# A written table in place of a greedy planner for the order of every engine

## The chip, the cores and the metric

The kernel runs on one core of one Trainium2 chip. The core has a matrix engine (PE, TensorE), a vector engine (DVE), an activation engine (ACT), a general engine (POOL, GpSimd) and a queue engine (SP). Each of them works through its own instructions in the order in which the program was written; they meet through semaphores. Matrix products land in PSUM, which has eight banks here: two for tiles named h, one each for y, u, x and z, and a pair named s. Before a bank can be used again, DVE or ACT has to copy its contents out ("evict" it).

The metric is the time of one execution on the device in microseconds, the median of several runs. Before the change it is 303.93 us (three runs, 302.88 to 303.95).

## What is computed

Attention with two kinds of sliding window, then a two-layer network with silu between the layers. Eight batches of 576 positions, eight heads of 64; the first four heads see the last 32 positions, the other four see every fourth of the last 128.

```python
def _attn_ref(q, k, v):
    scores = scale * np.matmul(q, k.transpose(0, 1, 3, 2))
    rel = pos[:, None] - pos[None, :]
    mask_plain = (rel >= 0) & (rel < 32)
    mask_dil = (rel >= 0) & (rel < 128) & (rel % 4 == 0)
    scores = np.where(masks[None], scores, -1e9)
    attn = softmax(scores)
    return np.matmul(attn, v)

def _moe_ref(x, w_in, w_out):          # x: 4608 x 512
    h = x @ w_in                       # 512 -> 2048
    g = h * (1.0 / (1.0 + np.exp(-h)))
    return g @ w_out                   # 2048 -> 512
...
x = attn_out.transpose(0, 2, 1, 3).reshape(4608, 512)
```

## The kernel before

The work is cut into 598 matrix steps and some steps without a product. The names below are those of the table in the change, and the prediction's steps can be found by them.

Attention, batch b of 8. Batches 0 to 2 load q and k in natural order and transpose them on PE (`trans_a`, `trans_b`, `trans_d` and their forms for batch 0: steps TA, TB, TD, TS, TR); batches 3 to 7 are cast into scratch memory by DMAs that POOL issues (`issue_cast`) and come back transposed by DMAs that SP issues (`issue_turn`, step T). `scores` (S, seven sets for the first three batches, six for the others) makes a block of scores in two banks, ACT takes the exp of it (L702 for a pair of banks in one instruction, L706 for each bank alone), and DVE multiplies by the mask (L712). In batch 0 the mask is added by a product with the identity (L681). `av_p` and `av_d` (P and D) multiply with v; DVE then takes a reciprocal and normalises (L742, L743). `x_p` and `x_d` (XP and XD) transpose the result into xA, the input of the network, and DVE or ACT copies it there (L571 on ACT, L573 on DVE). For batches 5 to 7 this transposition goes through memory and a DMA on SP (steps W and X). `vd_of` (V) copies v; `loads_gen` (L) issues the loads of a later batch behind two copies to a `fence` tile on POOL, which wait for the transposed loads of the batch before.

The network works on ten groups of tokens, two of 256 and eight of 512. `layer1` makes 16 pieces of 128 hidden channels for each group (steps l, L976). The eviction has two forms: a silu on ACT (L985), or a tanh on ACT (L988) with a product on DVE (L990). Exp and tanh share ACT's table; silu needs another, so a change from one to the other costs a table load. Groups 8 and 9 use Strassen's scheme with seven products of half size (`l1_fast`, L1078), and so does the second layer from group 2 on (`layer2_fast`, steps y with products 0 to 6, L1210; evictions at L1230, L1237 and L1240). The scheme needs sums of weights (`w_sums` and `w_last`, steps w and v; `wa_sums`, steps a, on POOL), of xA (`xt_sums`, t) and of the hidden values (`g_sums`, u, on DVE, for group 8 on POOL), at L1166 and L1027. The second layer of groups 0 and 1 is plain (`layer2`, L1130).

What sets the order is a planner in the kernel's own text. Each step is a generator that writes its products, then yields the name of an engine and an assumed time, and is sent on when that time has come in the plan. `Plan` keeps a clock for each engine and for each bank ring; `flush` decides between ACT and DVE ("ANY") by which would end first, and between tanh and silu ("L1") by which table is loaded. The main loop holds the attention's steps, the first layer's and the second layer's in three queues and picks at each point the first candidate that is ready, under limits on how far ACT and DVE may be behind:

```python
            r = max(r, plan.t + plan.backlog(it[1].uses) - lim)
            if r <= plan.t:
                pick = q_, it
                break
```

Assumed times for loads (`LOAD_US`, `AT_W0`) stand in place of their landings. Output tiles are stored by the ACT queue, from group 7 on by SP's (`BYSP`). The bank of a step is one of the free rings it may use; the second layer alternates between y and u.

Of the kernel before, what the change touches and what calls it, by code (L numbers as in the profile page):

```python
# [10 lines left out]
F32 = mybir.dt.float32  # L11
AF = mybir.ActivationFunctionType
# [4 lines left out]
def kernel(  # L17
# [43 lines left out]
    LOOK1 = 6  # L61
    BYSP = 7
    STAG = 2.5
# [4 lines left out]
    LOAD_US = {"w": 2.57, "o": 2.57, "d": 3.2, "p": 3.0, "r": 2.3, "v": 2.57, "k0": 2.2, "r0": 1.0, "v0": 2.3, "w0a": 1.3, "w0b": 1.3}  # L68
    AT_W0 = 11.4
# [3 lines left out]
    gtp = ctx.enter_context(tc.tile_pool(name="gtp", bufs=2))  # L73
    o32 = ctx.enter_context(tc.tile_pool(name="o32", bufs=2))
    obp = ctx.enter_context(tc.tile_pool(name="obp", bufs=3))
    dram = ctx.enter_context(tc.tile_pool(name="dram", bufs=1, space=bass.MemoryType.DRAM))
    ps_h = ctx.enter_context(tc.tile_pool(name="ps_h", bufs=2, space=bass.MemoryType.PSUM))
# [64 lines left out]
    pair_tmp = {  # L142
        "hh": [as32[0][:, HT * i : HT * (i + 1)] for i in range(4)] + [as32[2][:, :GT]],
        "xz": [as32[1][:, HT * i : HT * (i + 1)] for i in range(4)] + [as32[3][:, :GT]],
        "s": [as32[4][:, HT * i : HT * (i + 1)] for i in range(3)]
        + [as32[3][:, GT : GT + HT], as32[2][:, GT : 2 * GT]],
    }
# [126 lines left out]
    AT, AT_WIN = {}, {}  # L274
    at = AT_W0
    for what in ORDER:
# [24 lines left out]
        at += LOAD_US[what] if what in LOAD_US else LOAD_US[kind]  # L301
        AT[what] = at
        if kind == "w":
            for f in range(f0, f1):
                AT_WIN[4 * n + f] = at

    def third_batch():
        for n in range(2, PEB):
            issue_nat(n, 0, H)
        issue_vraw(2)  # L310
        issue_vp(2)
        issue_cast(PEB)
        yield "DMA", 0.0

    RINGS = {"h": 2, "y": 1, "u": 1, "s": 1, "x": 1, "z": 1}
    TABLE = 1.28
    HOP = 0.18
    OVER = {"ACT": 0.105, "DVE": 0.085}
    LAT = {"ACT": 0.15, "DVE": 0.125}
    SWITCH = 0.095  # L320
    LEAN = 0.1
    ORD = 1

    class Step:
        def __init__(self, make, pe, rings=(), deps=(), uses=()):
            self.make, self.pe, self.rings, self.deps, self.uses = make, pe, rings, deps, uses
            self.after = self.keep = self.done = self.mate = self.behind = None
            self.started = False
            self.freed = None
            self.mode = 128  # L330

    class Plan:
        def __init__(self):
            self.t = 0.0
            self.now = 0.0
            self.mode = 128
            self.free = {"ACT": 5.7, "DVE": 6.6, "POOL": 0.0}
            self.table = "exp"
            self.late = False
            self.soon = lambda: True  # L340
            self.sets = {}
            self.heap = []
            self.n = 0
            self.rings = {nm: [] for nm in RINGS}

        def push(self, step, gen, ready, value=None):
            self.now = ready
            try:
                eng, us = gen.send(value)
            except StopIteration:  # L350
                step.done = ready
                return
            heapq.heappush(self.heap, (ready, self.n, step, gen, eng, us))
            self.n += 1

        def flush(self):
            while self.heap and self.heap[0][0] <= self.t:
                ready, _, step, gen, eng, us = heapq.heappop(self.heap)
                if eng == "DMA":
                    heapq.heappush(self.heap, (ready + us, self.n, step, gen, "LANDED", 0.0))  # L360
                    self.n += 1
                    continue
                if eng == "LANDED":
                    self.push(step, gen, ready)
                    continue
                mode = None
                if eng in ("EXP", "L1", "SILU"):
                    mode = "silu" if eng == "SILU" else "exp"
                    if eng == "L1" and (self.table == "silu" or not self.soon()):
                        mode = "silu"  # L370
                    if mode == "silu" or eng == "EXP":
                        us += TABLE * (self.table != mode)
                        self.table = mode
                    eng = "ACT"
                if eng == "ANY":
                    ends = {e: max(ready, self.free[e]) + n for e, n in us.items()}
                    eng = min(ends, key=ends.get)
                    us = us[eng]
                hop = HOP
                if self.late:  # L380
                    us -= OVER.get(eng, 0.0)
                    hop = LAT.get(eng, HOP)
                end = max(ready, self.free[eng]) + us
                self.free[eng] = end
                self.push(step, gen, end + hop, mode or eng)

        def wait(self, step):
            wait = [d if isinstance(d, float) else d.done for d in step.deps]
            return None if None in wait else max(wait, default=0.0)

        def ready(self, step):
            wait = self.wait(step)
            if wait is None or step.behind and not step.behind.started:
                return None
            slots = [self.slot(nm) for nm in step.rings]
            slots = [x for x in slots if x is not None]
            if step.rings and not slots:
                return None
            return max(wait, min(slots, default=0.0))

        def slot(self, nm):
            done = [0.0]
            for c in set(nm):
                ring = self.rings[c]
                more = len(ring) - RINGS[c]
                done += [u.freed or u.done for u in ring[max(0, more) : max(0, more + nm.count(c))]]
            return None if None in done else max(done)

        def start(self, step):
            step.started = True  # L410
            self.t = max(self.t, self.ready(step))
            if step.pe and step.mode != self.mode:
                self.t += SWITCH
                self.mode = step.mode
            self.flush()
            ring = None
            if step.rings:
                slots = [(self.slot(nm), i) for i, nm in enumerate(step.rings)]
                ring = step.rings[min(x for x in slots if x[0] is not None)[1]]
                for c in ring:  # L420
                    self.rings[c].append(step.keep or step)
            self.t += step.pe
            self.push(step, step.make(ring), self.t + HOP + 0.02 * self.late)
            if step.after:
                step.after()

        def backlog(self, engs):
            return max((self.free[e] - self.t for e in engs), default=0.0)

    plan = Plan()  # L430
    t2 = at
    AT_DIL = {0: 6.1, 1: AT["d1"], 2: t2 + 7.0}
    AT_PLAIN = {0: 9.3, 1: AT["p1"], 2: t2 + 7.0}
    AT_VRAW = {0: 10.1, 1: AT["r1"], 2: t2 + 8.6}
    AT_VP = {0: 11.4, 1: AT["v1"], 2: t2 + 11.4}
    AT_CAST = t2 + 18.0
    AT_REST = AT["k0"]
    AT_V1 = AT["r0"]
    AT_VP1 = AT["v0"]
    AT_WOUT = [AT[f"o{n}"] for n in range(4)]  # L440

    POOLS = {"h": ps_h, "x": ps_x, "y": ps_y, "u": ps_y, "z": ps_z}
    readers = {}
    counts = {}

    def count(key, n, then):
        counts[key] = counts.get(key, 0) + 1
        if counts[key] == n:
            then()

    def at_t(then):
        plan.now = plan.t
        then()
# [50 lines left out]
    def loads_need(b):  # L504
        return 1 + (b > PEB or b == 3)
# [914 lines left out]
```

## Time and profile before

| | |
|---|---|
| median of three runs | 303.93 us |
| span of the profiled execution | 301.1 us |
| own time of the profiled execution outside its span | not shown; the median lies 2.8 us above this span |
| mean granted TensorE clock | 0.998 |
| PE, DVE, ACT, POOL busy | 289.0, 215.4, 194.7, 97.5 us |
| ACT table loads | 12, of 1.28 us each |
| output stores | 24 on ACT's queue, 12 on SP's |

The span goes from the first instruction to the last. A row of the windows gives a stretch, its length, then for each engine the busy time and the number of instructions, the granted clock, the share of the DMA engines' time and the rate. A row of the timeline or of the chain gives start, length, engine, line, tile and count; what stands in square brackets is the idle time before it and what ended it. The engines over time, in 40 equal slices and tenths:

```profile
PE   6889999989999999999999999999999999999995
...
DVE  6388999889957784768664787576667685599511
ACT  7677783478687766766765675667665496398320
POOL 8954814000640051005000669701600069800000
```

The attention of batches 0 to 2, with both small groups, fills about the first eleven slices; the Strassen groups of the first layer stand in slices 31 to 36.

### The profile page before, as it was taken

How to read it: one execution, taken by the hardware profiler on the slowest of the kernel's cores; microseconds unless marked ns; L12 is line 12 of the kernel's file. 1: busy time of each engine (PE TensorE's matmuls, PEld its weight loads, DVE VectorE, ACT ScalarE, POOL GpSimd, SP SyncE). 2: the span in 40 equal slices, each digit the busy share in tenths (PEclk: the TensorE clock that was granted, in tenths of full speed). 3: DMA queues.
4: the chain of work that ended last, by engine and by line, in shares of the span. 5: the costliest groups of instructions: out<-in, count | busy, mean ns of one | idle time of the engine just before them, and what ended most of it. 6: DMA issues, size and time to landing. Idle time of an engine off the chain costs nothing.

```text
span 301.1 us, 7429 instructions
## 1 busy us (share of the span) xinstructions
PE 289.0 (96%) x2922; PEld 203.6 (68%) x2922; DVE 215.4 (72%) x598; ACT 194.7 (65%) x427; POOL 97.5 (32%) x135
## 2 busy tenths in 40 slices
PE   6889999989999999999999999999999999999995
PEld 3558765644567666666775577568657888888884
DVE  6388999889957784768664787576667685599511
ACT  7677783478687766766765675667665496398320
POOL 8954814000640051005000669701600069800000
PEclk9999999999999999999999999999999999999999
DMA  7999999999999949897999999943113301200231
GB/s 106 184 199 198 202 192 193 209 203 190 95 159 186 218 68 167 164 219 107 168 268 181 151 195 246 223 81 111 54 30 106 111 2 64 77 2 0 90 121 72
DMA packets 100106, 42.26 MB, mean 140 GB/s; under 512 B 68584, under 2 KB 95464, under 8 KB 100072
## 3 DMA queue, kind: packets, MB, share of 16 engines
q0 software_dynamic: 48528, 19.86, 54.6%
q1 hardware_dynamic: 48088, 15.64, 26.6%
q10 hardware_dynamic: 3456, 6.29, 6.4%
q8 instruction: 23, 0.38, 0.5%
q14 instruction: 11, 0.09, 0.1%
HBM read 39.81 MB, written 17.10 MB: 189 GB/s over the span
## 4 chain that ended last, share of the span: by engine, by line
PE 81%; DVE 9%; ACT 4%; DMA 2%; issue 1%; POOL 1%; ACTq 0%; POOLq 0%
PE y L1210 30%; PE h L976 28%; PE h L1078 8%; PE y L1130 4%; PE s L693 3%; PE av_d L739 3%; DMA nat<-in_q_dram 2%; DVE gT L990 2%; PE av_p L739 2%; DVE probs L712 1%; ACT th L988 1%; DVE oP L743 1%; ACT probs L702 1%; PE xp L785 1%; DVE oD L743 1%
## 5 line engine op out<-in xcount | busy, mean ns | idle before, releaser
L976 PE MATMUL h<-xA,w_in 128*128 128x512 f16 (+1 forms) x512 | 110.4, 352 | 1.8 <-ACT probs L706 0.9
L985 ACT ACTIVATE gT<-h 128x512 f16<-128x512 f32 x84 | 49.6, 597 | 29.1 <-PE h L976 28.3
L976 PEld LDWEIGHTS <-w_in 128*128 128x128 f16 x512 | 45.2, 97 | 32.6 <-issue 2.5
L1210 PEld LDWEIGHTS <-gT 128*128 128x128 f16 x512 | 49.0, 98 | 7.3 <-issue 0.2
L1210 PE MATMUL y<-w_out,gT 128*128 128x256 f16 x384 | 48.2, 273 | 0.0
L1210 PEld LDWEIGHTS <-work 128*128 128x128 f16 x384 | 37.0, 98 | 7.1 <-issue 1.2
L1237 DVE TENSOR_TENSOR ob<-y,nat 128x256 f32<-128x256 f32 x48 | 20.1, 422 | 24.4 <-PE y L1210 18.5
L513 POOL COPY fence<-kqT 128x1 f16<-128x1 f16 x10 | 3.2, 329 | 93.2 <-DMA kqT<-kq_s 93.2
L1210 PE MATMUL y<-w_sum,work 128*128 128x256 f16 x256 | 32.0, 273 | 0.6 <-ACT nat L1230 0.6
L739 PEld LDWEIGHTS <-probs 128*128 128x128 f16 x448 | 22.9, 98 | 13.1 <-DVE oP L743 1.7
L702 ACT ACTIVATE probs<-s 128x768 f16<-128x768 f32 (+2 forms) x31 | 24.5, 791 | 6.4 <-PE s L693 3.6
L743 DVE TENSOR_TENSOR oD<-av_d,rcps 72x256 f16<-72x256 f32 x64 | 26.9, 421 | 2.2
L1230 ACT COPY nat<-y 128x256 f32<-128x256 f32 x48 | 18.0, 384 | 11.4 <-PE y L1210 10.1
L988 ACT ACTIVATE th<-h 128x256 f32<-128x256 f32 (+1 forms) x44 | 19.2, 445 | 7.4 <-PE h L976 4.7
L990 DVE SCALAR_TENSOR_TENSOR gT<-th,h 128x256 f16<-128x256 f32 (+1 forms) x44 | 20.6, 487 | 2.2 <-ACT th L988 2.1
L742 DVE RECIPROCAL rcps<-av_d 72x4 f32<-72x4 f32 x64 | 11.1, 173 | 14.8 <-PE av_d L739 14.7
L706 ACT ACTIVATE probs<-s 128x288 f16<-128x288 f32 (+2 forms) x40 | 18.6, 487 | 4.4 <-ACT ob L1240 1.3
L743 DVE TENSOR_TENSOR oP<-av_p,rcps 96x256 f16<-96x256 f32 x48 | 20.2, 421 | 1.6
L1240 ACT COPY ob<-y 128x256 f32<-128x256 f32 x16 | 5.9, 371 | 22.9 <-PE y L1210 20.3
L712 DVE TENSOR_TENSOR probs<-probs,mask_p 128x768 f16<-128x768 f16 x21 | 12.2, 584 | 10.3 <-ACT probs L702 7.5
L739 PE MATMUL av_d<-vd,probs 128*128 128x65 f16 x256 | 16.5, 194 | 0.6 <-ACT probs L706 0.3
L1210 PE MATMUL y<-w_out,work 128*128 128x256 f16 x128 | 16.6, 273 | 0.0
(129 smaller groups left out, 486.2 us busy)
## 6 DMA issues: line engine op xcount, KB each, us to landing
out_dram<-ob ACTq DMA_DIRECT2D x24, 256.0 KB, 4.7
out_dram<-ob SPq DMA_DIRECT2D x12, 256.0 KB, 2.0
kq_s<-in_k_dram POOLq DMA_DIRECT2D x5, 576.0 KB, 9.6
kq_s<-in_q_dram POOLq DMA_DIRECT2D x5, 576.0 KB, 13.6
vp<-in_v_dram POOLq DMA_DIRECT2D x7, 384.0 KB, 8.1
w_out<-in_moe_w_out_dram POOLq DMA_DIRECT2D x4, 512.0 KB, 10.4
vraw<-in_v_dram POOLq DMA_DIRECT2D x8, 224.0 KB, 5.4
w_in<-in_moe_w_in_dram POOLq DMA_DIRECT2D x3, 512.0 KB, 9.8
```

The lines of the kernel that those rows point to most:

```text
L702: nc.scalar.activation(p2, both[:, :, :n], AF.Exp, scale=scale)
L706: nc.scalar.activation(p2[:, i], sp[i][:, :n], AF.Exp, scale=scale)
L739: nc.tensor.matmul(a[:, i, : D + 1], lhs(i), rhs(i), start=True, stop=True)
L743: nc.vector.tensor_tensor(o, a[:n, :, :D], rcp[:n, :, None].broadcast_to([n, HN, D]), ALU.mult)
L976: nc.tensor.matmul(h[:, :w], w_in16[:, c, f * P : (f + 1) * P], x_g[:, c], start=(c == 0), stop=(c == HP - 1),)
L985: nc.scalar.activation(gTs[g][:, f, :w], h[:, :w], AF.Silu, scale=2.0)
L988: nc.scalar.activation(th[:, :w], h[:, :w], AF.Tanh)
L990: nc.vector.scalar_tensor_tensor(gTs[g][:, f, :w], th[:, :w], 1.0, h[:, :w], ALU.add, ALU.mult)
L1078: nc.tensor.matmul(y, lhs[:, c, j], rhs[:, c], start=first and c == 0, stop=c == 1, skip_group_check=not first,)
L1210: nc.tensor.matmul(y, lhs[:, c, tb * P : (tb + 1) * P], rhs[:, c], start=first and c == 0, stop=c == KP - 1, skip_group_check=not first,)
L1230: nc.scalar.copy((t1, t5, u2)[n], y)
L1237: nc.vector.tensor_tensor(half, y, (u2, t5, t1)[n - 3], ALU.add)
```

## The change

The planner goes: the class `Plan` with its clocks, rings and limits, the assumed times of loads, engines and hops, the three queues and the picking loop. In its place stands `TABLE`, a text of some 1,600 words, each the name of a step, with what it is given behind "=". The words are carried out from first to last:

```python
    for token in TABLE.split():
        name, _, what = token.partition("=")
        steps[name].go(what)
```

The first word of a step with products writes them, into the bank that it names (a and b are the two h banks, s the pair). Each further word lets the step write one more piece: an eviction on ACT (A) or DVE (D), a first-layer eviction as silu (s) or as tanh with a product (t), an output store on SP's queue (S) or else on ACT's. So the order of each engine, the bank, the evicting engine, the form and the queue are all written down. The start, the middle and the end of the table:

```diff
+TABLE = """
+0TD3=a 0TD2=y 0TD2=A 0TD3=D 0TD0=x 0TD1=b 0TD1=A 0TD0=D 0S3=s 0S4=yb 0S3 0S4 0S4 0TA1k=u 0TA1q=a 0TA0q=z
+0TA1k=A 0TA1q=A 0TA0k=b 0TA0k=A 0TA0q=A 0V0=A 0D01=x 0D01 0S1=au 0S1 0D00=x 0S1 0D00 0D03=z 0D02=a 0S0=s 0S0
...
+y1.1.2 y1.1.3 2TA1=y 2TA1=D 2TA1=D 2S5=s y1.1.3=A 2S6=za 2S6 2S6 2S5 2TA0=b 2TA0=D 2TB0=x 2TA1=D l2.2=u 2D03=z
...
+y9.0.6 y9.1.2 y9.1.3 y9.1.2=A y9.1.3 y9.1.4 y9.1.4 y9.1.5 y9.1.5 y9.1.5=S y9.1.6 y9.0.6=D y9.0.6=S y9.1.6=A
+y9.1.6=S
+"""
```

`Step` becomes a holder of its generator, and every `yield` loses its engine and time:

```diff
+        def go(self, what):
+            try:
+                if self.gen is None:
+                    self.gen = self.make(what)
+                    self.gen.send(None)
+                    if not self.pe:
+                        self.gen.send(None)
+                else:
+                    self.gen.send(what)
+            except StopIteration:
+                self.done = True
...
-            mode = yield "L1", 0.11 + w / 1200
+            mode = yield
-            if mode == "silu":
+            if mode == "s":
...
             if n < 3:
-                yield "ACT", 0.13 + DH / 1200
-                nc.scalar.copy((t1, t5, u2)[n], y)
+                eng = yield
+                copy_on(eng, (t1, t5, u2)[n], y)
...
             if n > 4:
-                (nc.sync if g >= BYSP else nc.scalar).dma_start(out=out[row : row + P], in_=ob)
+                eng = yield
+                (nc.sync if eng == "S" else nc.scalar).dma_start(out=out[row : row + P], in_=ob)
```

A step without products that copies (V, N) is carried on with nothing at its first word, so its copy is DVE's whatever the letter says. The four sums of `g_sums` become separate words, on POOL too, and so can stand apart:

```diff
+        eng = nc.gpsimd if g in ONPOOL else nc.vector
+        for args in ((S1, A21, A22, ALU.add), (A21, A11, A21), (S2, S1, A11), (S4, A12, S2)):
+            yield
+            minus(c, *args, eng=eng)
```

The scratch stores of batches 5 to 7 and the loads of the third batch, formerly written by the step that ended last (`x_stored`, `start_turn`, `start_loads`), become steps W, X, T, L and B of their own. Pools with two or three buffers become pools of one with a name for each buffer (gT0, gT1, th0, th1, ob0 to ob2), taken in turn as before. The two h banks get the names a and b, and any step may be given any bank that the table names.

In instructions: PE 2,922 products before and after. DVE gets 33 more entries in the list of instructions and ACT 35 fewer: 26 evictions of the second layer move from ACT to DVE; 84 silu evictions of 512 columns become 76, 12 tanh ones 20; 12 table loads become 18; 24 output stores on ACT become 11, 12 on SP 25. POOL's DMA issues keep their order among themselves.

More of the change, by code (lines that the diff above doesn't have):

```diff
@@ L1 @@
-import heapq
 from contextlib import ExitStack
@@ L300, with __init__ @@
             issue_vp(n)
[L301 to L305, printed above, removed]
+    class Step:
+        def __init__(self, make, pe):
+            self.make, self.pe, self.gen, self.done = make, pe, None, False
+        def go(self, what):
[9 more added lines that the diff above has]
+                self.done = True
@@ L307, in third_batch, with turn @@
+    steps = {}
+    turns = {"th": 0, "ob": 0}
+    def turn(nm, n):
+        turns[nm] += 1
+        return turns[nm] % n
     def third_batch():
+        yield
         for n in range(2, PEB):
             issue_nat(n, 0, H)
+        yield
         issue_vraw(2)
+        yield
         issue_vp(2)
+        yield
         issue_cast(PEB)
[L313 to L449, printed above, removed]
@@ L1235, in step @@
             if n < 6:
-                yield "DVE", 0.15 + DH / 960
+                yield
                 nc.vector.tensor_tensor(half, y, (u2, t5, t1)[n - 3], ALU.add)
             else:
-                yield "ACT", 0.13 + DH / 1200
-                nc.scalar.copy(half, y)
+                eng = yield
+                copy_on(eng, half, y)
             if n > 4:
-                (nc.sync if g >= BYSP else nc.scalar).dma_start(out=out[row : row + P], in_=ob)
-        steps = []
-        w3 = [w_steps["last", c] for c in WPARTS]
@@ L1279 @@
-    for g in range(FAST):
-        l2 += [(g, st) for st in layer2(g, [st for e, o in zip(even[g], odd[g]) for st in e + o])]
-    w_steps, sums = {}, []
-    for c in WPARTS:
-        w_steps["sums", c] = Step(
-            lambda ring, c=c: w_sums(c), 0.0, (), [max(AT_WOUT)], ("DVE",)
-        )
-        w_steps["last", c] = Step(
-            lambda ring, c=c: w_last(c), 0.0, (), [st for _, st in l2] + [w_steps["sums", c]], ("DVE",)
-        )
-    sums += [w_steps[key, c] for key in ("sums", "last") for c in WPARTS]
@@ L1290 @@
-    n = 0
-    for g in range(FAST, NG):
-        own = [
-            Step(
-                lambda ring, g=g, c=c: g_sums(g, c), 0.0, (),
-                sum(even[g][c[0] : c[1]] + odd[g][c[0] : c[1]], []), ("DVE",),
-            )
-            for c in (PARTS if g not in ONPOOL else PARTS_POOL)
-        ]
-        l2 += [(g, st) for st in layer2_fast(g, even[g], odd[g], own, n)]
-        n += HT // P
-        if g == B - 1:
-            sums += wa
-        sums += own
-    plan.push(Step(None, 0.0), first_cast(), 0.0)
@@ L1390 @@
-    plan.t += 100.0
-    plan.flush()
+                steps[f"y{g}.{tb}.{i}"] = Step(lambda ring, tb=tb, i=i: step(ring, tb, i), True)
+    for b in range(B):
+        attention(b)
+    for j in range(0, KP, 2):
+        steps[f"a{j}"] = Step(lambda ring, j=j: wa_sums(j), False)
+    for n, c in enumerate(WPARTS):
+        steps[f"w{n}"] = Step(lambda ring, c=c: w_sums(c), False)
+        steps[f"v{n}"] = Step(lambda ring, c=c: w_last(c), False)
+    for g in range(NG):
+        layer1(g)
+        if g < FAST:
+            layer2(g)
+            continue
+        layer2_fast(g)
+        for n, c in enumerate(PARTS if g not in ONPOOL else PARTS_POOL):
+            steps[f"u{g}.{n}"] = Step(lambda ring, g=g, c=c: g_sums(g, c), False)
@@ L1393 @@
+    for token in TABLE.split():
+        name, _, what = token.partition("=")
+        steps[name].go(what)
+    assert all(st.done for st in steps.values()), [nm for nm, st in steps.items() if not st.done]
 _INS = ['q', 'k', 'v', 'moe_w_in', 'moe_w_out']
```

634 lines of the change are left out of this document (221 added, 413 removed), and 24 rows, old and new, of the table order.

## The prediction

> **What bounds the kernel now.** I read the page first, then the chain of waits, the engines' windows, and the timeline where PE stood still.
>
> ```profile
> PE 289.0 (96%) x2922; PEld 203.6 (68%) x2922; DVE 215.4 (72%) x598; ACT 194.7 (65%) x427; POOL 97.5 (32%) x135
> ```
>
> PE looks full, but its ends are modelled, so the 96% hides small waits. The chain of waits (start, length, engine, line) gives PE's pace where nothing holds it:
>
> ```profile
> 47.52 3.45 PE y L1130 x16
> ...
> 159.19 1.73 PE h L976 x8
> ...
> 242.33 4.37 PE h L1078 x40
> 254.12 6.11 PE y L1210 x56
> ```
>
> A 512-wide product takes 3.45 / 16 = 0.216 us, a 256-wide one 6.11 / 56 = 0.109. By the counts of the groups that is (384 + 64) x 0.216 + (128 + 224 + 896) x 0.109 = 233 us for both layers. For the attention pieces I took the median distance from a piece's start to the next one's in PE's timeline (0.12 an av piece, 0.085 an xp, 0.26 an xd, 0.51 a td, 0.24 a score set, 0.7 one of batch 0): 44 us. So PE's own work from the first td on is 277 us. The span is 301.1; the first td starts at 5.3, the last matmul 3.9 before the end. That leaves 301.1 - 5.3 - 3.9 - 277 = 15 us in which PE waited, though the page shows 4% idle.
>
> Laying PE's steps in the order of before on that scale and reading their real starts says where: the first 10 us of own work took 14.7 (5.3 to 20.0), the next 60 took 66.6 (20.0 to 86.6), the 200.6 after that 204.6 (to 291.2). The windows show what differs (busy us in each stretch, in brackets the instructions):
>
> ```profile
> 20.00:86.60 66.60, 63.61 (x682) 40.24 (x684) 60.43 (x170) 45.11 (x105) 22.54 (x32) 1.00 1.36 185
> 86.60:291.20 204.60, 203.42 (x1986) 149.16 (x1986) 142.02 (x384) 133.59 (x286) 58.23 (x75) 1.00 0.71 126
> ```
>
> The third figure with brackets is DVE: 60.4 of 66.6 us (91%) in the early stretch, 142.0 of 204.6 (69%) later; ACT has room in both, 68% and 65%. So early on DVE sets the pace almost as much as PE, and its order matters. One place:
>
> ```profile
> 63.71 1.02 DVE L573 COPY work<-ta 128x384 f16<-128x384 f16 x2 [0.78 <-PE ta L582]
> ...
> 64.65 1.28 DVE L1166 TENSOR_TENSOR w_out<-w_out 128x1024 f16<-128x1024 f16 x2
> ```
>
> The two w_out differences (`w_last`, 0.68 each, not needed until product 4 of group 2) stand ahead of mask products and evictions just while PE loses 1.05 us. At the head it is a load:
>
> ```profile
> 8.02 0.42 PE L693 MATMUL s<-work 64*128 64x72 f16 x8
> 9.38 0.85 PE L643 MATMUL ta_q<-ident_w,nat 96*64 96x96 f16 x16 [0.94 <-DMA nat<-in_q_dram]
> ...
> 10.81 0.66 PE L681 MATMUL s<-mask_d,ident_w 128*128 128x288 f16 x2
> 11.40 0.30 PE L693 MATMUL s<-work 64*128 64x72 f16 x4
> ```
>
> PE waits for q from 8.2 to 9.4 and then does score set 4, which needs only what it had at 8.2.
>
> **What the change does, and its price.** PE's 598 steps are the same; 532 follow another step than before (median shift 1.4 us of PE's own work, up to 23), so the table is not the old order written down. Score excursions go from 32 to 33. At 0.1 to 0.15 us a switch (an 8-set costs 0.28 alone, 0.24 within a pair) that is 0.1.
>
> Head: set 4 stands right behind set 3. Its 0.95 us (10.81 to 11.75) fits the 1.18 us hole. What follows waits for four ACT copies of ta (0.50 each); ACT starts them near 10.0 as before, because set 4's two exps (0.44 each) fit between set 3's exp, ending at 9.1, and 10.0. Gain 0.9; bounds 0 (DVE holds it back) and 2 (batch 0's 14 normalisations, 0.55 each, start earlier and stay dense).
>
> Early stretch: I counted what DVE and ACT are given between PE's own 10th and 70th us, at the mean of the row of each form. DVE has 69.5 us of it before, 63.7 after: five differences of group 2's sums later (-2.7), tanh evictions of groups 1 and 2 down from 23 to 18 (-2.6), one w_out difference later (-0.7), tb, td and xd copies to ACT (-2.9), ta copies from ACT (+2.2), av and xp (+0.9). Rows overlap: the whole kernel's DVE sums to 236.0 by them and is busy 215.4, so 5.8 are 5.3 real. DVE's 60.4 becomes 55.1, below PE's 60.3. At the 91% that DVE reached before, 55.1 need 60.6, a gain of 6.0. ACT gets 4.5 more (four more table loads, less the copies): 45 to 49 of some 61, 80%, cover enough if no load stands ahead of a bank's eviction. Bounds 0 and 6.3 (all that PE lost there); I take 5.0, near the DVE row, less 1.0 for those loads.
>
> Later stretch: DVE is given 159.2 before and 180.9 after (26 evictions of y from ACT to DVE at 0.42, ten more tanh pairs at 0.68 on DVE, the sums moved here). Times 0.913 that is 19.9: 142.0 becomes 161.9, 79% of 204.6. PE lost 4.0 here. The upper bound of the gain is 4.0; the lower comes from the two rows: 2.0% lost at 69%, 10.4% at 91%, on the straight line 5.8% at 79%, 11.6 us, a loss of 7.6. I take a gain of 0.5, near the later row, because most added work (evictions of y) stands where the next product of the other bank, 0.87 us, covers a 0.42 us copy and its hops. One place is thin: group 8's sums on POOL. Nine of its operations (1.16 or 0.7 us) lie between what group 8 last delivers and product 2 of group 8; counted back it comes about 0.8 us late, which is in that 0.5.
>
> Table loads: 12 become 18, four more between PE's own 30 and 50, two near 190. What one costs shows here (ACT's timeline):
>
> ```profile
> 115.99 0.60 ACT L985 ACTIVATE gT<-h 128x512 f16<-128x512 f32 x1 [0.53 <-PE s L693]
> 116.60 1.28 ACT L702 ACT_TABLE_LOAD   x1
> 117.90 0.81 ACT L702 ACTIVATE probs<-s 128x768 f16<-128x768 f32 x1
> ```
>
> From the silu's end (116.59) to the exp's start 1.31 us: six are 7.9 us of ACT, which has 106 free. [...]
>
> Stores: 24 on ACT's queue and 12 on SP's become 11 and 25. Off ACT go 13 x 0.34 = 4.4 us of issue and its waits for DVE's half; on SP they stand among the transposing loads and wait there for ob. Bounds 0 and 13 x 0.33 = 4.3 if each delayed a needed load. I take 0: the loads' last landing (the POOL fence at 76.5, 109.3, 138.6, 166.8) is 5.7 to 10 us ahead of the batch's first scores (86.6, 115.6, 144.3, 174.1). Without that cover each late us is one of PE's. POOL's own DMA issues keep their order; only its sums change.
>
> Tail: the last step is still product 6, a copy on ACT and a store on SP, 3.9 us: nothing.
>
> Sum: 301.1 - 0.9 - 5.0 - 0.5 = 294.7 span. The median is 303.9 against this span, 2.8 more: 297.5.
>
> **Rivals.**
>
> *The early bound was not DVE* but the chain bank, exp, mask, av: then relief of DVE returns little, say 1.0, and the time is 303.9 - 0.9 - 1.0 - 0.5 = 301.5. For it: the wait at 64.90 ends on an ACT exp. Against it: DVE idle only 6.2 us in 66.6. Chance 0.17.
>
> *A fixed order wins nothing*: gains of 6 and new waits of 6 cancel, 303.5. For it: several steps follow their producer with almost nothing between. Chance 0.10.
>
> *DVE's work moved late becomes the bound there*, slower: the straight line's 7.6 against 5.9 won, 303.9 + 1.7 = 305.6. It decides once DVE passes some 80% in a stretch of 20 us behind 87. For it: 21.8 us of added rows. Against: ACT, not DVE, loses that work, and PE lost 2% there. Chance 0.09.
>
> *Table loads stand in PE's way*: six times 1.31 us with the early relief lost as well, 303.9 + 7.9 - 0.9 = 310.9. It decides where a bank waits behind a load for more than PE has ready; two of the new loads sit between batch 1's exps for a single silu. [...]
>
> *Nearly all waits vanish*: early 6.3, head 2, later 3: 292.6. Chance 0.08.
>
> **Numbers.** The forecast, 297.5, has 0.52, with a range of its own from 294.5 to 300.5. The range of 8 in 10 goes from 292.5 to 303.5: it leaves out the slower cases and half of the last. A difference under 0.5% (1.5 us) is no measurable change here, as the three runs spread by 1.1. Faster 0.52 + 0.17 + 0.08 = 0.77, same 0.10, slower 0.13.
>
> **What would show it.** Right: the stretch up to PE's own 70 us ends near 81 instead of 86.6, DVE under 56 us in it; no wait for q at 8.2; no stretch behind it where PE loses over 4%; 18 table loads of 1.28 with PE running beside them. Wrong: PE waits for ACT around 40 us, or for DVE's y evictions behind 87 us, or a batch's first scores wait for a transposing load.

## The result and the profile after

The changed kernel takes 299.9 us (four runs, 298.3 to 305.1) against 303.6 before: 0.988 of the time, with an interval of 0.983 to 0.992. A second set of six runs (299.0 to 306.6) gave 299.6 and 0.986 (0.983 to 0.989). The forecast was 297.5. Medians and ratios here and below leave out slow executions, those over 1.5% above the fastest of the same kernel, and the first profile (305.1, span 303.3) is of such a one, so that sizes are taken from the profile of the second set ("the repeat", 300.1, span 298.3). In every execution the time lies 1.7 to 1.9 us above the span.

The page of the changed kernel, first profile: busy times, then PE, DVE, POOL and the granted clock in 40 slices of 7.6 us.

```profile
PE 287.5 (95%) x2922; PEld 203.2 (67%) x2922; DVE 234.0 (77%) x632; ACT 190.1 (63%) x404; POOL 97.1 (32%) x135
...
PE   6899999999999999999999984999999999999994
...
DVE  6478988999897887787678889579768878578642
...
POOL 8854723002900520032000998000420025980000
PEclk9599999999999999999999999599999999999998
```

Where PE had only nines before, it now has an 8 and a 4, in slices 24 and 25; POOL is full beside them (9, 9, 8 in slices 23 to 25). The clock has a 5 in slice 2 and another in slice 26, behind PE's gap. DVE is up from 215.4 to 234.0.

The windows of the same profile (stretch, its length, then busy time and instructions of PE, PE's weight loads, DVE, ACT and POOL; clock, DMA share, rate). The first two rows are PE's own 10th to 70th and 70th to 160th us, the third reaches to the 180th:

```profile
19.60:81.20 61.60, 60.41 (x676) 38.50 (x676) 55.20 (x159) 47.84 (x107) 21.88 (x31) 1.00 1.35 192
81.20:172.10 90.90, 90.90 (x955) 62.28 (x954) 71.98 (x199) 59.00 (x113) 17.84 (x26) 1.00 1.08 171
172.10:202.00 29.90, 23.48 (x185) 13.73 (x183) 22.76 (x44) 11.76 (x22) 16.42 (x24) 0.89 0.98 160
```

The third stretch in the repeat, and the same before the change:

```profile
173.30:197.00 23.70, 20.75 (x185) 12.81 (x184) 19.58 (x45) 11.80 (x22) 16.04 (x23) 1.00 1.21 201
```

```profile
178.80:200.00 21.20, 20.80 (x185) 12.91 (x185) 15.08 (x41) 13.53 (x26) 14.71 (x21) 1.00 1.09 207
```

The early stretch, 66.6 us long before, now takes 61.6 with DVE at 55.2. In the next one PE shows no gap. In the third it stands still for 6.4 us of 29.9, in the repeat for 2.95 of 23.7, before the change for 0.4 of 21.2. The timeline there in the first profile, all engines in order of time:

```profile
183.28 6.22 DVE L653 TENSOR_TENSOR probs<-probs,mask_d 128x864 f16<-128x864 f16 x2
183.39 1.89 PE L805 MATMUL h<-xA,w_in 128*128 128x512 f16 x8
...
183.49 2.53 POOL L842 TENSOR_TENSOR nat<-nat,w_in 128x256 f16<-128x256 f16 x4
...
185.99 2.53 POOL L842 TENSOR_TENSOR kqT<-w_in,nat 128x256 f16<-128x256 f16 x4
...
189.43 0.68 DVE L819 SCALAR_TENSOR_TENSOR gT<-th,h 128x512 f16<-128x512 f32 x1
...
190.16 0.38 PE L680 MATMUL av_p<-vp,probs 128*128 128x65 f16 x4 [4.88 <-DVE gT L819]
```

Two mask products that take 0.60 each elsewhere take 6.22 together; the first of them alone took 5.70. It ends at 188.99, 0.47 behind the last of POOL's weight sums (`wa_sums`, L842), as if its own work began only then. The tanh product queued behind it on DVE holds a bank, and PE waits 4.88 us for it. In the repeat it is another DVE operation, 11 us earlier:

```profile
171.94 3.90 DVE L955 TENSOR_TENSOR gT<-gT 128x768 f16<-128x768 f16 x1
172.26 4.11 POOL L842 TENSOR_TENSOR nat<-w_in 128x256 f16<-128x256 f16 x6
...
176.83 0.60 PE L990 MATMUL y<-w_sum,work 128*128 128x256 f16 x4 [1.82 <-DVE nat L482]
```

This one takes 0.55 without POOL beside it. A stretched operation of this kind is not in the trace of before: there the sums run from 174.5 to 193.5, and no DVE operation with two operands in SBUF is longer by more than 0.5. Its longest meeting is this one, two mask products of 0.60 each that take 1.89 together:

```profile
176.76 6.19 POOL L1027 TENSOR_TENSOR nat<-w_in 128x256 f16<-128x256 f16 x7 [1.44 <-PE s L693]
...
180.54 1.89 DVE L712 TENSOR_TENSOR probs<-probs,mask_d 128x864 f16<-128x864 f16 x2
```

In the changed kernel it is no accident of one execution. All seven profiles of it and of its variants below in which POOL adds the weights without a pause have one DVE operation that ends 3 to 5 us late: the sum of hidden values of the repeat in four of them (3.05 to 3.36), the mask product of the first profile in two (5.11 and 5.12), another sum of hidden values in one (2.97). In the two other profiles with these sums on POOL, that of before and that of e9 with its pauses, none is longer by more than 0.5.

The table below says where time is won and lost in all runs. It is worked out as for the prediction: PE's steps are laid out on the scale of PE's own work, and the number is the real start minus that position, in us. What a row gains from one column to the next is what PE lost in that stretch. The positions are those of one profiled execution each; the last column is the median time.

| run | 0 | 10 | 70 | 160 | 190 | 270 | median |
|---|---|---|---|---|---|---|---|
| before | 5.3 | 9.9 | 16.3 | 18.8 | 20.1 | 20.6 | 303.6 |
| before, sums cut (e8) | 5.2 | 9.6 | 16.7 | 18.8 | 19.6 | 20.2 | 302.8 |
| changed, first profile | 5.2 | 9.6 | 11.2 | 12.1 | 22.1 | 22.3 | 299.9 |
| changed, repeat (e1) | 5.2 | 11.6 | 12.4 | 13.3 | 17.1 | 17.3 | 299.6 |
| sums cut (e2) | 5.2 | 11.3 | 12.7 | 13.6 | 13.8 | 14.0 | 295.8 |
| sums on DVE (e3) | 5.2 | 9.3 | 10.2 | 11.1 | 13.2 | 13.4 | 298.6 |
| four tanh (e4) | 5.2 | 12.6 | 15.7 | 16.6 | 21.1 | 21.3 | 302.5 |
| zeros between sums (e5) | 5.2 | 11.3 | 12.7 | 13.7 | 18.8 | 19.0 | 300.0 |
| set 4 moved back (e6) | 5.2 | 10.9 | 12.5 | 13.4 | 16.8 | 17.0 | 298.8 |
| stores on ACT (e7) | 5.3 | 10.1 | 11.2 | 12.2 | 15.7 | 15.9 | 299.8 |
| sums paced (e9) | 5.2 | 10.9 | 11.7 | 12.6 | 20.8 | 21.0 | 303.7 |
| sums on DVE, later (e10) | 5.2 | 10.6 | 11.5 | 12.4 | 12.6 | 14.4 | 297.1 |
| products added in the head (e11) | 5.2 | 8.7 | 11.4 | 12.3 | 20.9 | 21.1 | 305.3 |
| both (e12) | 5.1 | 8.6 | 10.2 | 11.1 | 11.8 | 13.0 | 296.7 |

Between 10 and 70 the kernel before loses 6.4 us (7.1 in e8), the changed one 1.6 and 0.8. Between 70 and 160 it is 2.5 against 0.9. Then the changed kernel gives back 10.0 and 3.8 us between 160 and 190, where before lost 1.3.

### The profile page after: what moved, and what is told of

Same layout as the page of the kernel before. It is cut to its first block, busy times and chain, and to the rows that moved or that the text cites. A ratio compares the mean times of both kernels' runs of the same rounds, so it can differ in the third digit from the quotient of the medians.

```text
span 303.3 us, 7398 instructions
## 1 busy us (share of the span) xinstructions
PE 287.5 (95%) x2922; PEld 203.2 (67%) x2922; DVE 234.0 (77%) x632; ACT 190.1 (63%) x404; POOL 97.1 (32%) x135
## 5 line engine op out<-in xcount | busy, mean ns | idle before, releaser
L805 PE MATMUL h<-xA,w_in 128*128 128x512 f16 (+1 forms) x512 | 113.2, 358 | 0.1
L814 ACT ACTIVATE gT<-h 128x512 f16<-128x512 f32 (+1 forms) x79 | 45.3, 591 | 45.1 <-PE h L805 44.9
L680 PEld LDWEIGHTS <-probs 128*128 128x128 f16 x448 | 25.3, 100 | 19.1 <-issue 6.6
L819 DVE SCALAR_TENSOR_TENSOR gT<-th,h 128x256 f16<-128x256 f32 (+1 forms) x49 | 24.6, 522 | 5.4 <-ACT th L817 5.2
L817 ACT ACTIVATE th<-h 128x256 f32<-128x256 f32 (+1 forms) x49 | 22.6, 480 | 8.8 <-PE h L805 6.2
L684 DVE TENSOR_TENSOR oP<-av_p,rcps 96x256 f16<-96x256 f32 x48 | 20.2, 421 | 1.6
L648 ACT ACTIVATE probs<-s 128x288 f16<-128x288 f32 (+2 forms) x40 | 16.9, 477 | 6.8 <-PE s L635 6.8
L683 DVE RECIPROCAL rcps<-av_d 72x4 f32<-72x4 f32 x64 | 11.1, 174 | 11.6 <-PE av_d L680 11.4
L653 DVE TENSOR_TENSOR probs<-probs,mask_d 128x576 f16<-128x576 f16 (+1 forms) x23 | 17.4, 769 | 2.2 <-ACT probs L644 2.1
L480 ACT COPY nat<-y 128x256 f32<-128x256 f32 x27 | 10.1, 381 | 13.9 <-PE y L990 13.6
L680 PE MATMUL av_p<-vp,probs 128*128 128x65 f16 x192 | 13.9, 195 | 5.2 <-DVE gT L819 4.9
L990 PE MATMUL y<-w_out,work 128*128 128x256 f16 x128 | 16.8, 273 | 1.0 <-DVE work L955 0.8
L680 PE MATMUL av_d<-vd,probs 128*128 128x65 f16 x256 | 17.3, 198 | 0.4 <-ACT probs L644 0.3
```

The lines of the kernel that those rows point to most:

```text
L648: nc.scalar.activation(p2[:, i], sp[i][:, :n], AF.Exp, scale=scale)
L653: nc.vector.tensor_tensor(p2, p2, mk, ALU.mult)
L680: nc.tensor.matmul(a[:, i, : D + 1], lhs(i), rhs(i), start=True, stop=True)
L684: nc.vector.tensor_tensor(o, a[:n, :, :D], rcp[:n, :, None].broadcast_to([n, HN, D]), ALU.mult)
L805: nc.tensor.matmul(h[:, :w], w_in16[:, c, f * P : (f + 1) * P], x_g[:, c], start=(c == 0), stop=(c == HP - 1),)
L814: nc.scalar.activation(gTs[g][:, f, :w], h[:, :w], AF.Silu, scale=2.0)
```

## The experiments

Each ran in the same set as runs of the kernel before; the ratios are against those.

**The changed kernel again (e1).** No edit.

> The changed kernel, nothing altered, to see whether the long DVE instruction of its profile comes back. In that profile (span 303.3 us) the kernel is 6.8 us ahead of the one before when PE has done 160 us of its own work, and 8 to 9 us are lost again between 160 and 181, where one mask product of 128x864 takes 5.70 us instead of 0.60 while POOL adds weights without a pause. Theory A (DVE and POOL get in each other's way while both read two tensors from SBUF, and how long depends on how they fall against each other): the times spread by several us, 298 to 305, and in a run of about 296.5 us span the mask products take at most 1.5 us each. Theory B (the profiled run was disturbed as a whole): the spread is that of the kernel before, about 1 us, and the place loses nothing.

299.6 (ratio 0.986, 0.983 to 0.989). The loss behind 160 is there again, with another size and at another operation, and all six runs together spread from 299.0 to 306.6.

**Without POOL's weight sums (e2).**

```diff
-            for c in range(2):
-                nc.gpsimd.tensor_tensor(
-                    o[:, c, j : j + 2], a[:, c, j : j + 2], b[:, c, j : j + 2], op
-                )
+            if j == 0:
+                for c in range(2):
+                    nc.gpsimd.tensor_tensor(o[:, c, :1, :8], a[:, c, :1, :8], b[:, c, :1, :8], op)
```

> The changed kernel without the sums of the first layer's weights on POOL (steps a; each is cut to 8 columns, so the half-size products of groups 8 and 9 read old data). Theory A: nothing is lost between 160 and 181 us of PE's own work, the span is 294 to 295, the ratio to the kernel before 0.970 to 0.975, the spread of its runs under 1.5 us. Theory B: same as the changed kernel, ratio 0.985 to 0.99, and the same spread.

295.8 (0.974, 0.971 to 0.977): 3.8 us less. From 160 to 190 PE loses 0.2 instead of 3.8; the window of the first 20 us of that stretch shows PE full and DVE at 75%:

```profile
173.60:194.00 20.40, 20.40 (x188) 13.26 (x187) 15.29 (x45) 12.12 (x22) 0.37 (x1) 1.00 1.30 210
```

So it is the sums that cost. They do it by way of DVE: in both profiles of the changed kernel every wait of PE in that stretch ends with a DVE operation, none with one of POOL. Why a DVE operation gets long beside POOL's sums the rows do not show. The runs still spread by 2.6 us, where under 1.5 was expected.

**The sums on DVE (e3).** Eight operations of 128x1024 in place of POOL's 32, at eight words between `y5.0.6` and `6W3`.

```diff
-                nc.gpsimd.tensor_tensor(
-                    o[:, c, j : j + 2], a[:, c, j : j + 2], b[:, c, j : j + 2], op
-                )
+            nc.vector.tensor_tensor(o[:, c], a[:, c], b[:, c], op)
```

> The changed kernel with the same weight sums on DVE, as eight instructions of 128x1024 (0.68 us each by the row of the sums of that size, 5.5 us) at places where DVE has room. Theory A: the 5.5 us of DVE are covered for the most part, PE loses at most 2 us in the stretch, span 294.5 to 297, ratio 0.972 to 0.980, faster than the changed kernel and with a smaller spread. Theory B: DVE's added work shows, ratio 0.990 to 1.005, slower than the changed kernel.

298.6 (0.981, 0.977 to 0.985). POOL does nothing from 170 to 230 us (0.00 busy in the windows), so no DVE operation meets a weight sum there. PE loses 2.1 us from 160 to 190 in place of 3.8, as DVE is given 4.1 us more there (six of the eight; the other two come at 209.5 and 212.8). By the medians that is 1.0 better than on POOL, though the intervals overlap at their ends, and it is not free.

**Four tanh evictions instead of silu (e4).** `l1.13`, `l1.14`, `l1.15` and `l2.0`, as in before; this takes four table loads away (18 become 14).

```diff
-l1.14=s
+l1.14=t l1.14
...
-l1.13=s l1.15=s
+l1.13=t l1.13 l1.15=t l1.15
...
-l2.0=s
+l2.0=t l2.0
```

> The changed kernel with pieces 13, 14 and 15 of group 1 and piece 0 of group 2 evicted by tanh and a product instead of silu: four table loads fewer around 37 to 60 us (4 x 1.28 = 5.1 us less of ACT), 3 x 0.42 + 0.68 = 1.9 us more of DVE, which is at about 90% there. If DVE sets the pace in the early stretch, as the forecast has it: 0.5 to 2 us slower by 70 us of PE's own work. If the table loads stand in PE's way: 1 to 5 us faster by that point.

302.5 (0.996, 0.993 to 0.999), 2.8 us slower. Between 10 and 70 PE loses 3.1 instead of 0.8; in the nine profiles of the changed kernel and its variants that leave this stretch alone and add nothing to the head, that number is 0.8 to 1.6. The windows of that stretch, e4 first and the repeat behind it:

```profile
22.60:85.70 63.10, 60.56 (x676) 38.67 (x676) 56.65 (x163) 42.80 (x103) 22.75 (x31) 1.00 1.38 184
```

```profile
21.60:82.40 60.80, 60.04 (x676) 38.55 (x676) 54.38 (x159) 47.68 (x106) 22.42 (x30) 1.00 1.36 190
```

DVE has 2.3 us more, ACT 4.9 less, and the stretch is 2.3 us longer, with DVE busy for 90% of it in e4, 89% in the repeat and 91% before the change. DVE sets the pace there; four table loads fewer on ACT bought nothing that shows beside it. (The profiled execution of e4 lies 4.1 above that of the repeat; the rest of this is a head later by 1.0 and 0.7 more behind 160.)

**A store of zeros between the sums (e5).**

```diff
                 nc.gpsimd.tensor_tensor(
                     o[:, c, j : j + 2], a[:, c, j : j + 2], b[:, c, j : j + 2], op
                 )
+                nc.gpsimd.memset(fence[:, 2:3], 0.0)
```

> The changed kernel, with a store of zeros into one unused column behind each of POOL's 32 weight sums: a POOL instruction that reads nothing, so that no two sums follow each other directly. Theory A (DVE is kept out over several sums because the next sum takes the place before DVE's waiting operation gets in): no DVE operation there is stretched by more than one sum, about 0.6 us; PE's loss between its own 160th and 190th us falls from 4.4 (repeat) and 10 (first profile) to 1 to 2, and the time falls from 299.7 to about 296.5, near the 295.8 without the sums. Theory B (the place changes hands at any rate only when POOL stops, or the sums' total time is what counts): the small stores change nothing or add to POOL's time, 299.7 to 301.

300.0 (0.990, 0.986 to 0.994): nothing won, as theory B had it. DVE's timeline still has an operation of 0.55 that takes 3.52:

```profile
174.85 3.52 DVE L954 TENSOR_TENSOR work<-work,gT 128x768 f16<-128x768 f16 x1
```

A POOL instruction of 0.09 us that reads nothing was no opening here; POOL never stood still in that time. Theory A fell in this form.

**The sums in pairs, POOL standing still between them (e9).**

```diff
             yield
+            nc.gpsimd.tensor_copy(fence[:, 2:3], gTs[6][:, done6.pop(0), :1])
             for c in range(2):
```

with the 16 words moved behind the 16 evictions of `l6`.

> The changed kernel with POOL's 32 weight sums in pairs, each pair held back by a one-column copy that waits for one eviction of group 6's first layer, so that POOL stands still between pairs. Theory A (DVE is let in when POOL stands still, and only then for certain): no DVE operation is stretched by more than two sums, 1.3 us; PE's loss between its own 160th and 190th us is 0.3 to 1.5 instead of 3.8 to 10; time 296 to 297.5. Theory B (the stretch doesn't depend on POOL's pauses): a DVE operation of 3 to 5 us is still there, and the time stays at 299.5 to 301.

303.7 (1.000, 0.998 to 1.002), so the time that theory A gave was far off. Its mechanism fits, though: in the seven profiles without pauses a DVE operation was held for about 3 us or more; here, in one profile, none beside a weight sum is longer by more than 0.5. The time went to a new wait: the paced sums end late, and score set 5 of batch 7, which stands behind them in the table and reads `kqT` too, waits for the last:

```profile
203.81 0.42 PE L633 MATMUL s<-kqT 64*128 64x72 f16 x8 [4.78 <-POOL kqT L843]
204.04 0.83 PE L633 MATMUL s<-nat 64*128 64x96 f16 x16
204.81 1.89 PE L991 MATMUL y<-w_sum,gT 128*128 128x256 f16 x8
```

The wait of 4.8 costs 8 us from 180 to 190, because the products behind it run at half rate for some 4 us: eight 256-wide ones take 1.89, where they take 1.04 elsewhere. The first profile shows the same behind its wait of 4.88, where eight 512-wide products take 3.45 instead of the 1.89 at 183.39:

```profile
192.71 3.45 PE L805 MATMUL h<-xA,w_in 128*128 128x512 f16 x8
```

That makes some 3 of the 7.8 us that it loses between 170 and 180.

**The sums on DVE, where it is idle (e10).** Eight operations of 128x1024 for four pieces each, seven of them between 209 and 223 us.

```diff
+        j0 = j // 4 * 4
...
+            nc.vector.tensor_tensor(
+                o[:, :, j0 : j0 + 4], a[:, :, j0 : j0 + 4], b[:, :, j0 : j0 + 4], op
+            )
```

> The changed kernel with the weight sums on DVE as eight operations of 128x1024 (0.68 us each by the row of that shape), seven of them placed between l6's end and the 220th us, where DVE is idle for 5 of 12 us in the run without the sums, and one at the 238th. If DVE's free time there covers them, PE loses nothing between its own 160th and 190th us and at most 0.5 behind, and the time is that of the run without sums, 295.8 to 296.5. If evictions wait behind them, PE loses up to 5.4 us of DVE work near its own 195th us: 297 to 300, no better than the first placing on DVE (298.6).

297.1 (0.979, 0.976 to 0.981). Nothing is lost from 160 to 190, 1.8 behind, more than the 0.5 hoped for: the longest wait (0.69, a bank for `l7`) stands behind three sums among batch 7's normalisations.

**Score set 4 back behind the transposing pieces (e6).**

```diff
-0S3=s 0S4=yb 0S3 0S4 0S4 0TA1k=u 0TA1q=a 0TA0q=z 0TA1k=A 0TA1q=A 0TA0k=b 0TA0k=A 0TA0q=A
+0S3=s 0S3 0TA1k=u 0TA1q=a 0TA0q=z 0TA1k=A 0TA1q=A 0TA0k=x 0S4=yb 0TA0k=A 0TA0q=A 0S4 0S4
```

> The changed kernel with score set 4 of batch 0 put back behind the four transposing pieces, as before the change. Theory A (as forecast: the set fills PE's wait for q): PE waits about 1 us for q again and everything behind comes 0.9 us later, 300.6. Theory B (what sets the head is when TensorE's products change from 80 to 43 ns, at 13.9 us before the change and at 15.4 or 20.3 in the runs of the changed kernel): the set's place matters less than that moment; if the pattern of work sets it, it comes near 14 again and the time falls by 0 to 2 us; if chance sets it, the repeated runs scatter over some 2.5 us as they did.

298.8 (0.985, 0.984 to 0.987): not 0.9 slower, but 0.8 faster, and the interval lies within that of the changed kernel. So the set's place is worth nothing that can be measured here. The rows that tell the head are the pairs of 384-wide mask products of batch 0, the same form at two rates. Before the change:

```profile
11.97 0.83 PE L681 MATMUL s<-mask_p,ident_w 128*128 128x384 f16 x2
...
13.16 0.50 PE L681 MATMUL s<-mask_p,ident_w 128*128 128x384 f16 x2
```

and in the repeat of the changed kernel:

```profile
13.54 0.83 PE L623 MATMUL s<-mask_p,ident_w 128*128 128x384 f16 x2
...
16.47 0.84 PE L623 MATMUL s<-mask_p,ident_w 128*128 128x384 f16 x2
```

In both profiles of the kernel before (the second is e8's), the full rate is there at 12.9 to 13.2 us; in nine profiles of the changed kernel and its variants with the same head it comes between 14.0 and 20.6. Five of the nine had it once before, up to about 8 us, and lost it (the 5 in slice 2 of the first profile's clock row). In e6 it comes between 14.7 and 17.1.

**Products added in the head (e11).** One more warm-up product and 13 of 128 columns with the identity, none of them read by anything, where PE waits for q and k. Four of the 13 stand behind one of the first transposing steps, without a word of their own; the other nine are the words 0K1 to 0K3.

```diff
+            for _ in range(n):
+                nc.tensor.matmul(t[:, :P], ident, ident, start=True, stop=True)
...
-0TD0=D 0S3=s 0S4=yb 0S3 0S4 0S4 0TA1k=u 0TA1q=a
+0TD0=D 0K1=u 0S3=s 0S4=yb 0S3 0S4 0S4 0K2=z 0TA1k=u 0K3=z 0TA1q=a
```

> The changed kernel with 14 products that nobody reads in the head: one more of the warm-up and 13 of 128 columns with the identity, in the holes in which PE waits for loads (5.3 to 6.2 and 7.5 to 10 us). Theory A (TensorE's half rate in the head hangs on how busy PE was just before): from the first td on, products take 43 ns and stay so, PE's own 10th us is reached at 18.5 to 19.5 instead of 19.3 to 21.6, and the time falls by 1 to 2 us with less scatter. Theory B (the moment of full rate doesn't depend on it): it still comes at 15 to 20 us, and the added products cost 0 to 1 us.

The head does as theory A says: full rate from the first pieces on, and PE's own 10th us at 18.7.

```profile
11.41 0.49 PE L634 MATMUL s<-mask_p,ident_w 128*128 128x384 f16 x2
```

Part of it is lost again at once in a wait of 1.4 us for `w_in` that ends at 24.6. The time is 305.3 (1.008, 1.005 to 1.011) all the same, with more scatter and not less (303.8 to 308.6): in its profile it is the mask product that is held (5.72 at 183.5), as in the first profile, and PE loses 8.6 us from 160 to 190, in the repeat 3.8. So a faster head went with the dearer of the two meetings. That the moment at which DVE and POOL arrive decides between them fits the rows; it was not tested.

**Both (e12).** The sums on DVE, two of them moved to about 183 and 194 us, and the added products.

> The weight sums on DVE as in the run before, two of them moved to the 183rd and 194th us, and the 14 added products in the head. Theory A (the two losses are separate: POOL against DVE behind PE's own 160th us, half rate in the head): PE's own 10th us is reached about 19 as in the run with the added products, nothing is lost between 160 and 190, at most 1.5 between 190 and 230, and the time is 295.5 to 296.5, under the 297.1 of the sums on DVE alone. Theory B (what the head gains is eaten by later loads, as the 1.4 us wait for w_in at 23 shows): PE's own 40th us comes no earlier than in the run before (52.0), and the time stays at 297.

296.7 (0.977, 0.975 to 0.979), 2.3% faster than before and 1% faster than the change. PE's own 40th us comes at 50.6 instead of 52.0 in e10's profile, and 0.7 is lost from 160 to 190. The median moved by only 0.4 against e10, less than the scatter of either: that the head's part is worth something in the end stands on one trace of each (14.4 against 13.0 by 270), not on the times.

**The stores of groups 0 to 7 back on ACT (e7).** Fifteen words lose their `=S`.

> The changed kernel with the 15 output stores of groups 0 to 7 that it gives to SP put back on ACT's queue. Theory A (as forecast, the stores' queue costs nothing on either side): 299.7 within 0.7. Theory B (SP's stores hold up transposing loads, or the loads hold up the stores and so the output buffers): the time falls by 1 to 3. Theory C (ACT was hurt by issuing and waiting for DVE's half): it rises by 1 to 3, and PE loses more between its own 100th and 230th us.

299.8 (0.987, 0.986 to 0.989): no difference.

**The kernel before without the sums (e8).** The same cut as in e2.

> The kernel before, with the weight sums cut to eight columns each, POOL's 32 sums of 256 gone: their result is missing, so groups 8 and 9 are computed with wrong sums. Theory A (the stretched DVE operations are a cost that the change brought): the kernel before loses little to them, 0.5 to 1.5 us of the 303.5, so 302.0 to 303.0. Theory B (both kernels pay for the sums, and the change only won elsewhere): 299 to 300.5. Its profile is also a second look at the head of the kernel before: with theory A of the head (chance) its products change to 43 ns at another moment than 13.9, with theory B at 13.9 again.

302.8 (0.998, 0.997 to 0.999): they cost it 0.8. The change brought 3.0 of the 3.8.

## The prediction, step by step

For the repeat the terms add up from the table: 301.1 + 1.7 (head) - 5.6 (10 to 70) - 1.6 (70 to 160) + 2.5 (160 to 190) - 0.3 (to 270) + 0.5 (tail) = 298.3, its span. The forecast's sum was 294.7. That the time came within 3 us of it is in part luck: the losses that it did not see, in the head and behind 160, met gains that it had put too low between 10 and 160.

**Early stretch: right, in cause and size.** 5.0 was forecast, 4.8 and 5.6 came; DVE was to have 55.1 and has 55.2 and 54.4; the stretch was to end near 81 and ends at 81.2 and 82.4. That DVE's load is the cause, and not the chain of the first rival, is shown by e4: 2.3 us of DVE work put back made the stretch 2.3 longer, 1.5 or more beyond the scatter.

**Table loads: right.** There are 18 of 1.28, and four fewer (e4) helped nothing; the rival that laid 7.9 us of them in PE's way, at a chance of 0.04, is not borne out. **Stores: right**, nothing by e7. The cover stood: no first scores of a batch wait for a transposing load.

**Head: wrong.** "Gain 0.9" by a set of products in a hole. The set does stand in it (in the repeat PE no longer waits for q, in the first profile 0.49 us of the wait is left), but what decides there is when TensorE comes to full rate. The step took every product's duration from before as given; in the changed kernel the same products ran at half rate for 2 to 7 us longer, and PE's own 10th us came 0.3 earlier to 1.7 later in the unedited kernel. Moving the set back doesn't restore it (e6). Which part of the head's order delays the full rate stays open; that it comes early with work in the holes is shown by e11 and e12 (0.49 for the first pair of mask products, at 11.41 and 10.88).

**Later stretch: the sign of DVE's load was judged right, the sums on POOL missed.** With DVE at 79% from 81 to 172, as worked out, PE lost 0.9 in place of 2.5: the straight line from 69% to 91%, which gave a loss of 7.6, does not hold there, and the rival of DVE as the late bound falls for that stretch. The step that failed is "POOL's own DMA issues keep their order; only its sums change": POOL's sums were costed as time on POOL (0.8 for group 8), not by what they do to DVE beside them. The weight sums themselves moved little (they begin at 174.5 before, at 171.7 and 172.3 after, which is some 3 to 4 us later in PE's own work), and DVE's own work beside them is no more: 15.1 us from 160 to 180 before, 15.3 in e2. What changed, by the rows, is which operations meet. Before, mask products and sums of hidden values, which read two operands from SBUF, stand beside POOL's sums only up to 184 us, and from there on DVE takes products out of PSUM; in the changed kernel such operations run beside the sums to 187 us and later. That this is what lets one be held is an inference: the sum held in the repeat stands at the very start of the weight sums, and before the change an operation of the same line met them there too (0.64 us at 174.8 in place of 0.28). The forecast's condition of no stretch behind 87 in which PE loses over 4% is not met: 2.95 of 23.7 us in the repeat.

**Tail: missed by 0.5.** In both kernels the last word is a store on SP behind product 6. But group 9's other half now ends late too (`y9.0.6=D`, `y9.0.6=S`), so that SP issues three stores there instead of two (start, length, count), and from the last eight products' start to the end it is 5.2 us instead of 4.7. That the third store makes the 0.5 was not tested. First before, then the repeat:

```profile
297.09 1.15 SPq L1242 DMA_DIRECT2D out_dram<-ob  x2
```

```profile
293.76 1.30 SPq L1022 DMA_DIRECT2D out_dram<-ob  x3
```

**The 2.8 around the span** is 1.8; before's profile is that of its fastest run, and the other 1.0 is that run's distance from the median.

## What to carry to other kernels

Where an engine off the critical path does long runs of elementwise work, cost it by what it does to its neighbour too (here 32 POOL sums, 3.8 us of the median), and look which of the neighbour's instructions will stand beside it after the change. A reordering changes those meetings even where the run itself hardly moves (174.5 before, 171.7 and 172.3 after), and one bad meeting can give back most of what a stretch has won, or more: here 3.8 and 10.0 us lost behind 160, against 5.6 and 4.8 won before 70. Read the rate of a form of product at several places before taking its duration as a constant (0.83 and 0.50 us for the same pair of mask products).

## What the hardware did that was not expected

**DVE held over many POOL instructions.** A DVE operation with two operands in SBUF that meets one or two POOL sums is mostly longer by 0 to 0.5 us (0.47 again and again in the changed kernel), less than one sum (0.66). But the 0.55 operation of the repeat had begun 0.32 before POOL's first sum and ended 3.35 us late, across five sums and into a sixth, and the one of the first profile 5.1 late, across eight. So to start first did not keep that operation from being held, and five of POOL's sums ended beside it without its coming to an end. With a copy of 0.18 to 1.33 us on POOL between the pairs of sums it didn't occur (e9, one profile), with a store of 0.09 us between the sums it did (e5), and before the change it didn't, though mask products met sums there too. What picks the operation that is held was not found.

**Half rate for long.** PE's products in the head ran at half rate up to 20 us although PE was busy from 8 us on (e1: 1.91 to 2.00 of every 2.00 us from 7 to 19), and the granted clock in the rows reads 1.00 all the while; only the products' durations show it. The last of these rows:

```profile
17.00:19.00 2.00, 2.00 (x26) 1.05 (x26) 0.96 (x3) 1.05 (x3) 1.35 (x4) 1.00 1.37 203
```

Where the full rate had been there once and was lost, the same column does read 0.50 (first profile, 9 to 13 us). The half rate came back behind PE's waits of 4.78 us (e9) and 4.88 us (first profile), and the full rate came early in e11, where added products stand in PE's waits for loads. But work alone did not bring it in the repeat: PE was busy for 11.8 of the 12 us from 7 to 19, with narrow products at half rate. What sets the moment was not found.
